# Pooled attention and a residual MLP on one core: where batch 1's v and u go, and when batch 2 is loaded

## The chip, the cores and the metric

The kernel runs on one core of a Trainium2 chip. The metric is the device time of one execution in microseconds (us). Names used below: PE is TensorE (matmuls), DVE is VectorE, ACT is ScalarE, POOL is GpSimd, SP is the engine that issues most DMA. A DMA issued by SP or ScalarE goes out in queue q1 or q10 of the profile, one issued by GpSimd in q0.

## What is computed

Eight batches, eight heads, 576 positions, head size 64. k and v are averaged over groups of 8 positions, so each head has 72 pooled keys and values. The attention's output, heads side by side, is the input x (576 x 512) of a residual MLP that first mixes positions with w_tok and then channels with two weights.

```python
k_p = k.reshape(B, H, 72, 8, D).mean(axis=3)
v_p = v.reshape(B, H, 72, 8, D).mean(axis=3)
attn = softmax(q @ k_p.transpose / sqrt(D))
x = heads_side_by_side(attn @ v_p)

a1 = alpha1 * x + beta1
u = x + lam * einsum('ts,bsd->btd', w_tok, a1)
a2 = alpha2 * u + beta2
out = u + lam * (maximum(a2 @ w_ch1, 0) @ w_ch2)
```

## The kernel before

The 576 positions of a batch make four chunks of 128 rows and one of 64; the 64 of two neighbouring batches share a chunk. Four chunks make a block of the MLP, and there are nine blocks. Blocks and attention are interleaved by hand: while block n runs, the attention and the mixing of batch n + 1 run too, and the loads of batch n + 2 are issued. A block is a list of steps with a number that fixes their order: `mlp_A` (first weight, 16 pieces, steps 0 to 15) and `mlp_B` (second weight, steps 16 to 31), and between them everything else. Block 0 also holds the end of the setting up.

```python
chunks = []
for b in range(0, B, 2):
    chunks += [(b, c) for c in range(4)]
    chunks += [(b + 1, c) for c in range(4)]
    chunks += [(b, 4)]
```

Batch 1's v comes in as 16-bit numbers (cast by the DMA), and TensorE pools it with a matrix of ones and zeros. From batch 2 on v comes in as fp32 and VectorE pools it with three additions for a pair of heads.

```python
def first_V(b, u, copy=nc.vector.tensor_copy):
    ...
    for c in range(4):
        nc.tensor.matmul(out=vp, lhsT=pool_v, rhs=main[:, heads, c], ...)
    for c in range(2):
        nc.tensor.matmul(out=vp, lhsT=pool_vr, rhs=rest[:, heads, c], ...)
    for r in range(2):
        copy(out=vp1_pool[2 * u + r][:, :, 0:64], in_=...)

def att_V(b, hp):
    t = st1[b]["v"][hp // 2][:, 2 * (hp % 2):2 * (hp % 2) + 2]
    for n in (4, 2):
        nc.vector.tensor_tensor(out=t[:, :, 0:n], in0=t[:, :, 0:n], in1=t[:, :, n:2 * n], op=ALU.add)
    nc.vector.tensor_tensor(out=vp1_pool[hp][:, :, 0:64], in0=t[:, :, 0], in1=t[:, :, 1], op=ALU.add)
```

k is summed by GpSimd in two steps (`sum_k`), and TensorE then makes the pooled keys (`att_K`, tile ps_kp, copied to kp). The scores (`att_S4`) need kp and the transposed q.

u is needed with channels on the partitions. For batches 0 and 1 TensorE transposes it and ScalarE copies it to u_fm; later batches use a DMA transpose (the crossbar) from SP.

```python
def mix_uT(key):
    ...
    if key[0] > 1 or key == (0, 4):
        nc.sync.dma_start_transpose(out=u_fm[blk][:, :, 128 * at:128 * at + 128], in_=s["u_bf"])
        return
    ps_uT = gp("ps_uT").bitcast(BF)
    for cc in range(4):
        nc.tensor.transpose(out=ps_uT[0:P, 128 * cc:128 * cc + 128], ...)
    nc.scalar.copy(out=u_fm[blk][:, :, 128 * at:128 * at + 128], ...)
```

The 64 remaining positions of odd batches need the last rows of the transposed w_tok on other partitions than those of even batches. Before, TensorE transposes that part a second time:

```python
def setup_wtok_odd():
    ps_w = gp("ps_wo").bitcast(BF)
    for tcx in range(5):
        nc.tensor.transpose(out=ps_w[:, P * tcx:P * tcx + trc], ...)
    nc.scalar.copy(out=wtT[:, 5, 0:S], in_=ps_w[:, 0:S])
    nc.scalar.copy(out=wtT[0:1, 5, 0:S], in_=wtT[64:65, 4, 0:S])
```

Batch 2's loads are held back by small VectorE memsets into their tiles ("gates"), whose place in VectorE's order sets when SP may issue them.

Of the kernel before, what the change touches and what calls it, by code (L numbers as in the profile page):

```python
# [9 lines left out]
BF = mybir.dt.bfloat16  # L10
# [4 lines left out]
P = 128  # L15
# [4 lines left out]
REM = 64  # L20
# [3 lines left out]
def kernel(  # L24
# [18 lines left out]
    nc = tc.nc  # L43
    ctx.enter_context(tc.manual_schedule())
    B, H, S, D = q.shape
# [6 lines left out]
    def gp(name):  # L52
        return psA.tile([P, 512], FP, tag="gp", name=name)
# [70 lines left out]
                    in_=src[b, h::2, 512:576, :].rearrange("a (i c) d -> i a (c d)", c=2))  # L124
        st1[b]["rem_raw"] = raw

    def load_v(b, u, parts=(0, 1), behind=None):

        if parts[0] == 0:
            st1[b]["v"][u] = work.tile([SPG, 4, 8, D], FP, tag="v_u", bufs=2, name="v_u")  # L130
        v_u = st1[b]["v"][u]
        if behind is not None:
            for rows_ in (slice(0, 64), slice(64, SPG)):
                behind.memset(v_u[rows_, 0, 0, 0:1], 0.0)
        for part in parts:
            g0, g1 = ((0, 64), (64, SPG))[part]
            nc.sync.dma_start(
                out=v_u[g0:g1].rearrange("g h p d -> g h (p d)"),
                in_=v[b, 4 * u:4 * u + 4, 8 * g0:8 * g1].rearrange("h (g p) d -> g h (p d)", p=8))

# [171 lines left out]
        nc.scalar.copy(out=wtT[64:65, 4, cols], in_=ps[64:65, 0:trc])  # L312

    def setup_wtok_odd():
        ps_w = gp("ps_wo").bitcast(BF)
        for tcx in range(5):
            trc = P if tcx < 4 else REM
            nc.tensor.transpose(out=ps_w[:, P * tcx:P * tcx + trc],
                                in_=wt_bf[0:trc, S * tcx + 448:S * tcx + 576],
                                identity=identity_bf[0:trc, 0:trc])  # L320
        nc.scalar.copy(out=wtT[:, 5, 0:S], in_=ps_w[:, 0:S])
        nc.scalar.copy(out=wtT[0:1, 5, 0:S], in_=wtT[64:65, 4, 0:S])


    w1 = [const.tile([P, 4, 512], BF, tag=f"w1_{g}", name=f"w1_{g}") for g in range(4)]
# [5 lines left out]
    def load_w1(g):  # L331
        nc.gpsimd.dma_start(
            out=w1[g],
            in_=moe_w_ch1[:, 512 * g:512 * g + 512].rearrange("(cc p) j -> p cc j", p=P))
# [249 lines left out]
    def mix_uT(key):  # L584
        s = st2[key]
        i = where[key]
        blk, at = i // 4, i % 4
        if blk not in u_fm:
            u_fm[blk] = work.tile([P, 4, 512], BF, tag="u_fm", bufs=3, name="u_fm")
        if key[0] > 1 or key == (0, 4):  # L590
            nc.sync.dma_start_transpose(out=u_fm[blk][:, :, 128 * at:128 * at + 128],
                                        in_=s["u_bf"])
            return
        ps_uT = gp("ps_uT").bitcast(BF)
        for cc in range(4):
# [126 lines left out]
    setup_wtok(3, nc.scalar.copy)  # L722
    att_X(0, 6, 8, nc.vector, False)
    rest_X(0, 0, H)
    load_w1(3)
    load_v16(1, (0, 1))
    mix_T(0, 0, nc.gpsimd)
    setup_rowsum(2)
    mix_T(0, 1)
    setup_rowsum(3)  # L730
    load_v16(1, (2,))
    load_w2(0)
    mix_T(0, 2, nc.gpsimd)
    for g in range(1, 3):
# [16 lines left out]
    def attention(b):  # L751


        first = b == 1
        todo = []
        if first:
            for hp in range(4):
                todo.append((2.6 + 0.9 * hp, lambda hp=hp: att_F(b, hp)))
            todo.append((3.5, lambda: cast_rem(b, nc.gpsimd)))
            todo.append((3.65, lambda: load_w2(3)))  # L760
            todo.append((7.4, lambda: att_Frem(b, nc.scalar.copy)))
        if b < B - 1:
            at = 27.0 if first else 10.0
            todo.append((at, lambda: att_F(b + 1, 0)))
            todo.append((at + 0.1, lambda: att_F(b + 1, 2)))
            at = 28.0 if first else 25.5
            todo.append((at - 1.0, lambda: cast_rem(b + 1, nc.gpsimd)))
            todo.append((at, lambda: att_Frem(b + 1)))
        for u in range(2):
            todo.append((3.6 + 0.1 * u if first else -0.9 + 1.2 * u,  # L770
                         lambda u=u: sum_k(b, u, nc.gpsimd)))
            todo.append((6.4 + 1.8 * u if first else 4.1 + 2.0 * u,
                         lambda u=u: att_K(b, u, nc.vector.tensor_copy)))
            if first:
                todo.append((11.0 + 1.2 * u, lambda u=u: first_V(b, u)))
        for u in range(2):
            at = (9.0 if first else 6.3, 13.6)[u]
            todo.append((at, lambda u=u: att_S4(b, u)))
            for k, dt in enumerate((0.1, 0.1, 0.1, 0.7, 1.7, 1.75) if u else (0.1, 0.1, 0.1, 1.1, 2.1, 3.1)):
                todo.append((at + dt, lambda u=u, k=k: st1[b]["exp", u](k)))  # L780
            for i, dt in enumerate((2.9, 3.4, 4.6, 5.1) if u else (5.7, 6.2, 2.9, 3.4)):
                h = 4 * u + i
                todo.append((at + dt, lambda h=h: att_AV(b, h)))
                if i % 2:
                    eng = nc.gpsimd if h == 5 else nc.vector
                    todo.append((at + dt + 0.1, lambda h=h, eng=eng: att_X(b, h - 1, h + 1, eng)))
        if not first:
            for hp in range(4):
                todo.append((0.2 + 2.0 * hp, lambda hp=hp: att_V(b, hp)))
        for c in range(5):  # L790
            at = 21.0 + 1.3 * c
            if c < 4 or b % 2:
                todo.append((at, lambda c=c: mix_T(b, c)))
                key = (b, c) if c < 4 else (b - 1, 4)
                if first and c in (2, 3):
                    at += 1.3 * c - 2.0
                elif first and c < 2:
                    at += 1.0
                todo.append((at + 1.8, lambda key=key: mix_uT(key)))
        return todo  # L800

    for n in range(NBLK):
        todo = []
# [16 lines left out]
        if b < B:  # L820
            todo += attention(b)
            if b + 1 < B:
                new_batch(b + 1)
                gate = nc.vector if b == 1 else None
                for u in range(2):
                    at = 21.0 + 0.2 * u
                    todo.append((at, lambda b=b, u=u: load_k(b + 1, u, gate)))
                    at = (21.0 if b == 1 else 0.4) + 0.1 * u
                    todo.append((at, lambda b=b, u=u: load_q_bf(b + 1, u)))
                    at = 19.0 + 0.2 * u if b == 1 else 3.5 + 4.0 * u  # L830
                    todo.append((at, lambda b=b, u=u: load_v(b + 1, u, behind=gate)))
                todo.append((20.9, lambda b=b: load_rem(b + 1, behind=gate)))
        for _, do in sorted(todo, key=lambda x: x[0]):
            do()

# [29 lines left out]
```

The softmax here doesn't subtract the row's maximum and nothing guards it: scores larger than these inputs give would overflow.

## Time and profile before

| what | value |
|---|---|
| time, median of 3 runs | 349.15 us (348.95 to 349.62) |
| span of the profiled execution | 347.7 us |
| TensorE busy | 336.4 us, 97% |
| VectorE busy | 219.8 us, 63% |
| ScalarE busy | 150.3 us, 43% |
| GpSimd busy | 89.7 us, 26% |
| DMA moved | 44.57 MB |
| granted TensorE clock | 1.00 |

How to read what follows. The page shows the span in 40 equal slices with a digit of busy share for each engine. In a group or a timeline a line gives the start and the busy time in us, the engine, the line of the kernel, the operation, output and inputs by their tiles, shapes, and the count; square brackets hold the idle time just before it and what ended that. In a table of stretches each line has the stretch, its length, then busy time and number of instructions for PE, weight loads, DVE, ACT and POOL, then the granted clock, the mean busy share of the DMA engines and GB/s. Matmuls are pipelined, so the distance from one start to the next says more of their cost than their own duration.

### The profile page before, as it was taken

The page shows a single profiled execution, that of the slowest core. Times are in us where ns is not written, and L with a number is a line of the kernel's source. Part 1 is how long each engine was busy: PE and PEld are TensorE (multiplying, and loading weights), DVE is VectorE, ACT ScalarE, POOL GpSimd, SP SyncE. Part 2 cuts the span into 40 slices and gives each one's busy share as a digit, 9 for nine tenths or more (in the row PEclk, how much of TensorE's full clock was granted, in tenths as well). Part 3 has the DMA queues.
Part 4 walks back from the last instruction along what each step waited for, and adds up shares of the span by engine and source line. Part 5 has one row for each costly group of instructions (what it writes and reads, how often), then busy time and mean ns, then how long its engine had stood idle before and what let it go on. Part 6 is the DMA issues. An engine that isn't in the chain of part 4 may idle for free.

```text
span 347.7 us, 5897 instructions
## 1 busy us (share of the span) xinstructions
PE 336.4 (97%) x2208; PEld 178.9 (51%) x2249; DVE 219.8 (63%) x463; ACT 150.3 (43%) x283; POOL 89.7 (26%) x104
## 2 busy tenths in 40 slices
PE   8999999998999999999999999999999999999995
PEld 3667554454545554455445544554455445545544
DVE  6673159788686669775867597858685882037511
ACT  3656970257403850186018700790079005604700
POOL 8677404080117011800180027101600100000000
PEclk9999999999999999999999999999999999999999
DMA  8999953999558924895289628991820134011012
GB/s 123 184 219 243 214 115 44 239 240 196 93 178 152 222 48 112 216 201 86 77 235 175 113 72 208 197 139 53 221 69 1 37 85 77 0 60 62 0 58 63
DMA packets 66045, 44.57 MB, mean 128 GB/s; under 512 B 32409, under 2 KB 57309, under 8 KB 66018
## 3 DMA queue, kind: packets, MB, share of 16 engines
q1 hardware_dynamic: 50484, 33.18, 40.2%
q0 software_dynamic: 15072, 10.76, 21.1%
q8 instruction: 17, 0.28, 0.3%
q10 hardware_dynamic: 462, 0.27, 0.3%
q14 instruction: 10, 0.08, 0.1%
HBM read 38.30 MB, written 9.44 MB: 137 GB/s over the span
## 4 chain that ended last, share of the span: by engine, by line
PE 89%; DVE 4%; POOL 2%; DMA 2%; issue 2%; ACT 1%; POOLq 0%; DVEq 0%
PE ps_ch L646 34%; PE ps_h L612 33%; PE ps_tok L575 12%; PE ps_av L521 2%; PE ps_s L477 2%; DMA q_bf<-in_q_dram 2%; DVE v_u L445 1%; PE ps_ch L635 1%; DVE ps_ch L652 1%; PE ps_r L484 1%; PE ps_uT L596 1%; PE ps_av L525 1%; PE ps_kp L407 0%; PE ps_q L370 0%; DVE u_sb L653 0%
## 5 line engine op out<-in xcount | busy, mean ns | idle before, releaser
L617 ACT ACTIVATE Hj<-ps_h,bias_cols 128x512 bf16<-128x512 f32 x144 | 98.4, 689 | 149.1 <-PE ps_h L612 147.6
L612 PE MATMUL ps_h<-u_fm,w 128*128 128x512 bf16 (+1 forms) x571 | 132.2, 374 | 1.3 <-ACT u_fm L598 0.2
L646 PE MATMUL ps_ch<-w,Hj 128*128 128x512 bf16 x543 | 128.7, 379 | 1.1 <-issue 0.6
L612 PEld LDWEIGHTS <-w 128*128 128x128 bf16 x592 | 63.9, 114 | 51.8 <-issue 2.9
L646 PEld LDWEIGHTS <-Hj 128*128 128x128 bf16 x560 | 52.7, 98 | 61.0 <-issue 1.6
L575 PE MATMUL ps_tok<-xs,wtT 128*128 128x512 bf16 (+2 forms) x199 | 44.8, 380 | 0.5 <-DVE xs L543 0.2
L652 DVE TENSOR_TENSOR ps_ch<-lam_bc,ps_ch 128x512 f32<-128x512 f32 x32 | 22.2, 693 | 35.0 <-PE ps_ch L646 34.7
L543 POOL TENSOR_TENSOR xs<-x_tm,lamal_bc 128x512 bf16<-128x512 f32 x10 | 12.7, 1268 | 118.5 <-DVE x_tm L529 115.9
L579 DVE TENSOR_TENSOR u_sb<-x_tm,ps_tok 128x512 f32<-128x512 f32 (+1 forms) x40 | 27.4, 684 | 12.2 <-PE ps_tok L575 12.1
L529 DVE TENSOR_TENSOR x_tm<-ps_av,rec 128x320 f32<-128x320 f32 x64 | 31.4, 491 | 2.8
L653 DVE TENSOR_TENSOR u_sb<-u_sb,ps_ch 128x512 f32<-128x512 f32 x35 | 24.0, 687 | 13.7 <-PE ps_ch L646 12.5
L506 ACT ACTIVATE ET<-ps_s 72x512 f16<-72x512 f32 x56 | 32.3, 592 | 0.0
L527 DVE RECIPROCAL rec<-ps_av 128x5 f32<-128x5 f32 x64 | 12.2, 191 | 31.7 <-PE ps_av L525 31.6
L445 DVE TENSOR_TENSOR v_u<-v_u 72x512 f32<-72x512 f32 (+1 forms) x48 | 28.4, 591 | 0.8
L575 PEld LDWEIGHTS <-wtT 128*128 128x128 bf16 (+3 forms) x200 | 17.4, 100 | 20.9 <-issue 1.3
L582 DVE TENSOR_TENSOR u_bf<-u_sb,al_bc 128x512 bf16<-128x512 f32 x34 | 24.2, 711 | 1.3 <-DMA u_fm<-u_bf 0.2
L160 POOL TENSOR_TENSOR k_raw<-k_raw 128x512 f32<-128x512 f32 x14 | 19.3, 1376 | 11.9 <-DMA k_raw<-in_k_dram 9.4
L521 PEld LDWEIGHTS <-ET 72*128 72x128 f16 x256 | 13.9, 97 | 8.6 <-issue 0.4
L162 POOL TENSOR_TENSOR k_bf<-k_raw 128x512 bf16<-128x512 f32 x14 | 17.8, 1274 | 1.1
L543 DVE TENSOR_TENSOR xs<-x_tm,lamal_bc 128x512 bf16<-128x512 f32 x22 | 15.4, 701 | 0.7
L521 PE MATMUL ps_av<-vp,ET 72*128 72x66 f16 x256 | 15.8, 193 | 0.0
L145 POOL CAST rem_q<-rem_raw 128x256 bf16<-128x256 f32 x7 | 2.8, 399 | 42.0 <-DMA rem_raw<-in_q_dram 42.0
(121 smaller groups left out, 229.9 us busy)
## 6 DMA issues: line engine op xcount, KB each, us to landing
out_dram<-u_sb SPq DMA_DIRECT2D x32, 256.0 KB
k_raw<-in_k_dram SPq DMA_DIRECT2D x14, 512.0 KB
v_u<-in_v_dram SPq DMA_DIRECT2D x12, 512.0 KB
q_bf<-in_q_dram POOLq DMA_DIRECT2D x16, 256.0 KB, 6.5
w<-in_moe_w_ch_dram POOLq DMA_DIRECT2D x8, 512.0 KB, 16.3
v<-in_v_dram POOLq DMA_DIRECT2D x4, 256.0 KB, 11.2
rem_raw<-in_q_dram SPq DMA_DIRECT2D x15, 64.0 KB
rem_raw<-in_k_dram SPq DMA_DIRECT2D x15, 64.0 KB
```

Of the source, the lines that this page charges most:

```text
L445: nc.vector.tensor_tensor(out=t[:, :, 0:n], in0=t[:, :, 0:n], in1=t[:, :, n:2 * n], op=ALU.add)
L506: nc.scalar.activation(out=o, in_=i, func=AF.Exp, bias=0.0, scale=0.125)
L521: nc.tensor.matmul(out=av[:, odd + c, :], lhsT=ET[:, m0:m0 + 128], rhs=vp1[:, hh, :])
L529: nc.vector.tensor_tensor(out=x[:, 1 - odd:6 - odd, dd:dd + D], in0=av[:, :, 0:64], in1=rec.unsqueeze(2).to_broadcast((P, 5, D)), op=ALU.mult)
L543: eng.tensor_tensor(out=xs[:, 0:4, cols], in0=x[:, 1:5, cols], in1=lamal_bc[:, cols].unsqueeze(1).to_broadcast((P, 4, D * (h1 - h0))), op= ...
L575: nc.tensor.matmul(out=ps_tok[p0:p1], lhsT=wtT[0:kk, at, P * c:P * c + p1 - p0], rhs=xs_pool[i][0:kk, sc, :], start=(sc == 0), stop=(sc == 4))
L579: nc.vector.tensor_tensor(out=s["u"][p0:p1, :], in0=x[p0:p1, 1 + c if c < 4 else 5 - 5 * i, :], in1=ps_tok[p0:p1, 0:DM], op=ALU.add)
L582: eng.tensor_tensor(out=s["u_bf"], in0=s["u"], in1=al2_bc, op=ALU.mult)
L612: nc.tensor.matmul(out=ps_h[:, t0:t1], lhsT=w1_of(cc, j), rhs=u_fm[n][:, cc, t0:t1], start=(cc == 0), stop=(cc == 3))
L617: nc.scalar.activation(out=t, in_=ps_h, func=AF.Relu, bias=bias_cols[:, j:j + 1], scale=1.0)
L646: nc.tensor.matmul(out=ps, lhsT=Hj[n, j][:, 128 * m:128 * m + 128], rhs=w2[j // 4][:, j % 4, :], start=(j == 0), stop=(j == NJ - 1))
L652: nc.vector.tensor_tensor(out=ps, in0=lam_bc, in1=ps, op=ALU.mult)
```

## The change

It has four parts. Batch 1's v is loaded as fp32 by GpSimd's queue, ahead of w1's last piece, and pooled by VectorE (`att_V`) like all later batches; `first_V` stays for batch 0 alone. Batch 1's u goes over the crossbar, like all later batches. The odd w_tok rows are moved by two small DMAs from SP instead of being transposed a second time. Batch 2's loads (q, v, the remainders, k) are issued from the middle of block 0, where they were issued late in it, and its transposes of q move from step 27 to step 21.5. It is meant to take work off TensorE in block 0 and to use the time in which the DMA engines have little to do.

```diff
-    def load_v(b, u, parts=(0, 1), behind=None):
+    def load_v(b, u, parts=(0, 1), behind=None, queue=nc.sync):
...
     def setup_wtok_odd():
-        ps_w = gp("ps_wo").bitcast(BF)
-        for tcx in range(5):
-            trc = P if tcx < 4 else REM
-            nc.tensor.transpose(out=ps_w[:, P * tcx:P * tcx + trc], ...)
-        nc.scalar.copy(out=wtT[:, 5, 0:S], in_=ps_w[:, 0:S])
-        nc.scalar.copy(out=wtT[0:1, 5, 0:S], in_=wtT[64:65, 4, 0:S])
+        nc.vector.memset(wtT[0:64, 5, 0:S], 0.0)
+        nc.sync.dma_start(out=wtT[64:128, 5, 0:S], in_=wtT[0:64, 4, 0:S])
+        nc.sync.dma_start(out=wtT[0:1, 5, 0:S], in_=wtT[64:65, 4, 0:S])
...
-        if key[0] > 1 or key == (0, 4):
+        if blk:
             nc.sync.dma_start_transpose(out=u_fm[blk][:, :, 128 * at:128 * at + 128],
...
-    load_w1(3)
-    load_v16(1, (0, 1))
+    for u in range(2):
+        load_v(1, u, queue=nc.gpsimd)
     mix_T(0, 0, nc.gpsimd)
     setup_rowsum(2)
     mix_T(0, 1)
     setup_rowsum(3)
-    load_v16(1, (2,))
+    load_w1(3)
     load_w2(0)
...
-            at = 27.0 if first else 10.0
+            at = 21.5 if first else 10.0
             todo.append((at, lambda: att_F(b + 1, 0)))
             todo.append((at + 0.1, lambda: att_F(b + 1, 2)))
-            at = 28.0 if first else 25.5
+            at = 25.5
             todo.append((at - 1.0, lambda: cast_rem(b + 1, nc.gpsimd)))
             todo.append((at, lambda: att_Frem(b + 1)))
...
-            todo.append((6.4 + 1.8 * u if first else 4.1 + 2.0 * u,
+            todo.append((6.4 + 2.2 * u if first else 4.1 + 2.0 * u,
                          lambda u=u: att_K(b, u, nc.vector.tensor_copy)))
-            if first:
-                todo.append((11.0 + 1.2 * u, lambda u=u: first_V(b, u)))
...
-        if not first:
-            for hp in range(4):
-                todo.append((0.2 + 2.0 * hp, lambda hp=hp: att_V(b, hp)))
+        for i, hp in enumerate((1, 0, 2, 3) if first else range(4)):
+            todo.append(((6.6, 8.7, 10.0, 12.6)[i] if first else 0.2 + 2.0 * hp, lambda hp=hp: att_V(b, hp)))
...
-                if first and c in (2, 3):
-                    at += 1.3 * c - 2.0
-                elif first and c < 2:
-                    at += 1.0
                 todo.append((at + 1.8, lambda key=key: mix_uT(key)))
...
-                    at = 21.0 + 0.2 * u
+                    at = (15.2 if b == 1 else 21.0) + 0.2 * u
                     todo.append((at, lambda b=b, u=u: load_k(b + 1, u, gate)))
-                    at = (21.0 if b == 1 else 0.4) + 0.1 * u
+                    at = (14.0 if b == 1 else 0.4) + 0.1 * u
                     todo.append((at, lambda b=b, u=u: load_q_bf(b + 1, u)))
-                    at = 19.0 + 0.2 * u if b == 1 else 3.5 + 4.0 * u
+                    at = 14.5 + 0.2 * u if b == 1 else 3.5 + 4.0 * u
                     todo.append((at, lambda b=b, u=u: load_v(b + 1, u, behind=gate)))
-                todo.append((20.9, lambda b=b: load_rem(b + 1, behind=gate)))
+                todo.append((15.1 if b == 1 else 20.9, lambda b=b: load_rem(b + 1, behind=gate)))
```

More of the change, by code (lines that the diff above doesn't have):

```diff
@@ L136, in load_v @@
             g0, g1 = ((0, 64), (64, SPG))[part]
-            nc.sync.dma_start(
+            queue.dma_start(
                 out=v_u[g0:g1].rearrange("g h p d -> g h (p d)"),
@@ L314, in setup_wtok_odd @@
     def setup_wtok_odd():
-        ps_w = gp("ps_wo").bitcast(BF)
-        for tcx in range(5):
-            trc = P if tcx < 4 else REM
-            nc.tensor.transpose(out=ps_w[:, P * tcx:P * tcx + trc],
-                                in_=wt_bf[0:trc, S * tcx + 448:S * tcx + 576],
-                                identity=identity_bf[0:trc, 0:trc])
-        nc.scalar.copy(out=wtT[:, 5, 0:S], in_=ps_w[:, 0:S])
-        nc.scalar.copy(out=wtT[0:1, 5, 0:S], in_=wtT[64:65, 4, 0:S])
+        nc.vector.memset(wtT[0:64, 5, 0:S], 0.0)
+        nc.sync.dma_start(out=wtT[64:128, 5, 0:S], in_=wtT[0:64, 4, 0:S])
+        nc.sync.dma_start(out=wtT[0:1, 5, 0:S], in_=wtT[64:65, 4, 0:S])
     w1 = [const.tile([P, 4, 512], BF, tag=f"w1_{g}", name=f"w1_{g}") for g in range(4)]
```

## The prediction

> **What bounds the kernel now.** I read the page's busy shares and slices first, then TensorE's time block by block, then the waits and the timelines of the first 80 us, where every change lies.
>
> ```profile
> PE 336.4 (97%) x2208; PEld 178.9 (51%) x2249; DVE 219.8 (63%) x463; ACT 150.3 (43%) x283; POOL 89.7 (26%) x104
> ...
> DMA  8999953999558924895289628991820134011012
> ```
>
> TensorE is nearly always busy, so only less work on it, or less waiting by it, saves time. A slice is 8.7 us. The DMA engines are full to about 43 us, fall to 5 and 3 tenths between 43 and 61 us (in the records the last w2 piece lands at 50.2, and nothing moves from then until batch 2's first load), and are full again to 87 us: a hole in front of the loads that the change brings forward.
>
> The table of stretches has one block of the MLP per line; each starts at its first ps_h matmul (blocks 0 to 4).
>
> ```profile
> 28.53:71.80 43.27, 42.33 (x345) 24.90 (x349) 22.74 (x54) 22.30 (x46) 12.31 (x15) 1.00 0.89 179
> 71.80:108.39 36.59, 35.18 (x221) 18.10 (x224) 27.47 (x52) 15.24 (x28) 14.19 (x14) 1.00 0.79 164
> 108.39:144.88 36.49, 36.12 (x230) 18.49 (x234) 27.55 (x55) 15.09 (x28) 9.66 (x11) 1.00 0.66 146
> 144.88:180.09 35.21, 35.00 (x222) 18.09 (x224) 24.70 (x52) 15.09 (x28) 9.34 (x10) 1.00 0.67 149
> ```
>
> Blocks 1 and 3 do the same work, yet block 1 takes 36.59 and block 3 35.21: **1.38 us** are lost in block 1, the most that earlier loads of batch 2 can give there. Blocks 2 and 4 (36.49 each) need nothing. VectorE's timeline shows how it is lost, and TensorE's where.
>
> ```profile
> 73.34 3.12 DVE L445 TENSOR_TENSOR v_u<-v_u 72x512 f32<-72x512 f32 x2
> 76.49 1.25 DVE L447 TENSOR_TENSOR vp<-v_u 72x128 f16<-72x128 f32 x1
> 77.66 1.13 DVE L445 TENSOR_TENSOR v_u<-v_u 72x512 f32<-72x512 f32 x2
> ```
> ```profile
> 36.50 0.28 PE L407 MATMUL ps_kp<-pool_main,k_bf 128*128 128x64 bf16 x4
> ...
> 39.48 0.29 PE L407 MATMUL ps_kp<-pool_main,k_bf 128*128 128x64 bf16 x4 [0.28 <-POOL k_bf L162]
> ...
> 79.53 0.30 PE L477 MATMUL ps_s<-qT,kp 64*72 64x256 bf16 x2 [1.19 <-DVE kp L419]
> ```
>
> Pooling the first half-pair of v takes 3.12 + 1.25 us beside GpSimd's sums of k (GpSimd is busy from 71.88 to 77.6); the next pair takes 1.13 + 0.29. So kp is copied late and the scores wait 1.19 us. The first two TensorE lines are batch 1's pooled k in block 0: the first half does not wait at all, the second 0.28 us for GpSimd. Keep them in mind.
>
> GpSimd's queue there, with the DMA issues in it, and the time to landing of two earlier loads (x1: q of batch 1, second half, issued at 11.65; w1's third piece, issued at 14.03):
>
> ```profile
> 28.28 0.60 POOL L337 DMA_DIRECT2D w<-in_moe_w_ch_dram  x1
> 29.55 0.53 POOL L337 DMA_DIRECT2D w<-in_moe_w_ch_dram  x1 [0.68 <-DMA q_bf<-in_q_dram]
> 30.07 0.41 POOL L145 CAST rem_q<-rem_raw 128x256 bf16<-128x256 f32 x1
> 30.44 0.73 POOL L148 TENSOR_TENSOR rem_k<-rem_raw 128x256 bf16<-128x256 f32 x1
> 32.62 1.27 POOL L160 TENSOR_TENSOR k_raw<-k_raw 128x512 f32<-128x512 f32 x1 [1.45 <-PE ps_h L612]
> 33.97 1.27 POOL L162 TENSOR_TENSOR k_bf<-k_raw 128x512 bf16<-128x512 f32 x1
> ```
> ```profile
> q_bf<-in_q_dram POOLq DMA_DIRECT2D x1, 256.0 KB, 17.6
> ...
> w<-in_moe_w_ch_dram POOLq DMA_DIRECT2D x1, 512.0 KB, 19.5
> ```
>
> The issue at 29.55 (w2's third piece) waited for that q: 11.65 + 17.6 = 29.25. That q is the eighth load before it in this queue, and the one wait of w1's third piece (1.59 us, at 14.03) was also for its eighth forerunner. **An issue on this queue waits until the load eight places earlier has landed**, and all that stands behind it on GpSimd waits too.
>
> [...]q1 (SP) with 40.2% and q0 (GpSimd) with 21.1% are shares of one set of 16. [...] 3.12 against 1.13 us above, and GpSimd's 1.27 becomes 1.71 at 74.46.
>
> **The change part by part.** First what leaves TensorE in block 0. Starts of neighbours in its timeline give the true cost:
> - the odd w_tok transposes: 39.66 to 40.11, **0.45 us**;
> - first_V of batch 1, two times six matmuls: 43.56 to 44.43, and 46.09 to 46.95, **1.73 us**;
> - u of batch 1, four sets of four transposes of 0.22 us: **0.87 us**.
>
> That is 3.05 us. ScalarE loses 0.64 + 0.67 (wtT copies) and 4 x 0.59 (u_fm). Second, block 1: batch 2's v gates move from step 19 to 14.5 and k from 21 to 15.2, so some 8 us earlier. Its sums of k, at 71.9 to 77.6 now, should be done before block 1 begins, VectorE pools at 1.4 us a pair, and I take **1.3 of the 1.38 us** as won.
>
> Third, what it adds. VectorE pools v for batch 1: four pairs of 1.13 + 0.29 = 5.7 us, plus a memset; in 28.7 to 51.3 us it was busy only 5.92 of 22.6, so this fits, though one pair will meet GpSimd's sum of k and take 2 to 3 us. The loads: v as fp32 is 4 issues where there were 3. Counting places as built, w2's first three pieces now wait for q, q and **w1's third piece** where the third waited for q. w1's third piece lands at 14.03 + 19.5 = 33.5. So GpSimd, free at 30.08 before, is free at about 34.1: cast 0.41, remainder 0.73, sum 2 x 1.27 with gaps, k_bf at 37.9 instead of 35.2. TensorE wants it at 36.50: **a stall of 1.4 us**. Then w2's fourth piece is issued (0.57), and the second sum ends at 41.1, or 41.6 beside VectorE; TensorE would come there at 40.6: another 0.5 to 1.0. Less the old 0.28, I count **2.0 us** for both.
>
> Fourth, ScalarE in the score stretch (41 to 52 us) has about 9 us of copies and exps; without first_V TensorE's own work there is about 9 too. I charge **0.4 us** of lost pace.
>
> Fifth, the crossbar. Block 1 is the only block whose four chunks are all of the batch mixed just before, so it needs all four u of batch 1. In a steady block SP's four u transposes take 1.2 us each among other issues (173.05 to 180.2) and the last lands 1.2 us later. Here SP must first issue v, rem and k of batch 2 from about 50 us. In the steady blocks v's landing comes some 10 us after its first issue (149.36, then 159.1), so near 60.5, and SP then issues one output, two q transposes, u, output, u, u, rem, u: about 10 us, with the last u landing near 71.5. TensorE comes at 71.8 - 3.05 + 2.0 + 0.4 = 71.2, or later. I charge **0.7 us**, from 0 to 2.
>
> w1's and w2's last pieces come about 1 us later than now (fp32 v has twice the bytes of the cast one): w1's fourth near 41.5, needed at 45; w2's fourth near 51.5, needed at 53.8. No wait expected.
>
> Sum: -3.05 - 1.3 + 2.0 + 0.4 + 0.7 = **-1.25 us**, so 349.15 becomes about 347.9.
>
> **Rivals.** (a) All saved work counts and no new wait comes: -4.35 us, 344.8. For it: the parts are tuned together (the second k half is moved from 8.2 to 8.6). Against it: the queue order, which the trace has shown to bind twice. (b) The crossbar chain becomes the bound at block 1's start: the last u lands at 74 or so, 2 to 3 us later than TensorE comes, and the time is 350. For it: SP's issues are serial and the k loads stand in front; against it: nothing moves the SP work later than 50 us. (c) v and q of batch 2 take bandwidth from the last w2 pieces, and the first ps_ch sums wait: 1 to 2 us, 349. For it: q of batch 2 is ungated on GpSimd and goes out near 42 us; against it: it stands behind w2 in the same queue.
>
> **Range and chances.** The removed work (3.05) is near certain, block 1's gain nearly so; the stalls have 0 to 6 us between them. 345.5 to 350.0 holds most of it. A change of 2% is 7 us, more than the whole of the saved work: faster by that 0.01, slower by it 0.02.
>
> **What will show it.** A wait of GpSimd for a w load before rem_q, and ps_kp waiting some 1.4 us for k_bf near 37 us: the third step. Block 1 at 35.3 us or so, with no wait for kp: the second. A gap of TensorE before block 1's first ps_h, released by a DMA: the fifth. If GpSimd does not stop there, or if w1's third piece lands before 31 us, I am too high by 2; if the last u lands after 73 us, too low.

## The result and the profile after

The changed kernel takes **362.04 us** (median of 4 runs, 361.70 to 362.89), the kernel before, run beside it, 349.38 (348.95 to 349.94). The ratio is 1.0365, 95% interval 1.0341 to 1.0389: slower by 3.6%, where 347.9 was predicted and 350.0 was the top of the range. In this part, where a kernel's runs spread widely, ratios are taken over its undisturbed runs and medians over all of them.

The page after, first the busy shares, then the granted TensorE clock and the DMA share in the 40 slices (a slice is 9.0 us now):

```profile
PE 341.4 (95%) x2176; PEld 180.0 (50%) x2216; DVE 223.8 (62%) x472; ACT 147.0 (41%) x277; POOL 89.8 (25%) x105
...
PEclk9969969998999999999999999999999999999999
DMA  8999991999243892489459926694650033002002
```

TensorE has 32 matmuls fewer and yet 5.0 us more busy time: the clock's row, all 9 for the kernel before, has two slices at 6 and one at 8. The table of stretches, one line per block (blocks 0 to 2), shows where the time went:

```profile
31.44:85.15 53.71, 42.30 (x313) 23.17 (x316) 31.56 (x71) 18.84 (x40) 19.64 (x21) 0.94 0.94 185
85.15:122.04 36.89, 36.68 (x221) 18.38 (x226) 21.53 (x45) 15.17 (x28) 6.48 (x7) 0.95 0.48 119
122.04:158.53 36.49, 36.17 (x232) 18.50 (x234) 27.29 (x55) 15.10 (x28) 9.68 (x11) 1.00 0.67 143
```

Block 0 starts 2.91 us later than before, takes **10.44 us more**, block 1 takes 0.30 more, and block 2 takes what it took (36.49). TensorE's timeline has three long gaps in block 0 (the last is counted to it, as it lies ahead of block 1's first matmul):

```profile
42.38 0.29 PE L402 MATMUL ps_kp<-pool_main,k_bf 128*128 128x64 bf16 x4 [2.80 <-POOL k_bf L162]
...
49.08 0.39 PE L402 MATMUL ps_kp<-pool_main,k_bf 128*128 128x64 bf16 x4 [3.98 <-POOL k_bf L162]
...
85.15 6.17 PE L607 MATMUL ps_h<-u_fm,w 128*128 128x512 bf16 x20 [4.00 <-DVE v_u L440]
```

The third is put down to VectorE, but in the DMA's own records the last crossbar transpose of u lands at 84.90 us, 0.25 us before TensorE goes on; that is what it waited for. Whose fault the first two are, GpSimd's timeline shows:

```profile
33.73 0.53 POOL L332 DMA_DIRECT2D w<-in_moe_w_ch_dram  x1 [1.94 <-DMA w<-in_moe_w_ch_dram]
...
39.72 1.26 POOL L160 TENSOR_TENSOR k_raw<-k_raw 128x512 f32<-128x512 f32 x1 [4.36 <-DMA k_raw<-in_k_dram]
...
46.44 1.25 POOL L160 TENSOR_TENSOR k_raw<-k_raw 128x512 f32<-128x512 f32 x1 [3.60 <-DMA k_raw<-in_k_dram]
```

The first line is the stop on w1's third piece that the prediction told of. But it isn't what ends last: GpSimd then waits 4.36 us and 3.60 us **for k itself**. Both halves of k, issued 2 us later than before (24.9 and 25.5, before 22.6 and 23.2), landed at 39.7 and 46.4 us; before they landed at 32.5 and 36.7.

The granted clock stood at half in three stretches: one ahead of block 0, one that begins in the second gap, and one from the end of the third gap on. The last three columns of a stretch's line are the clock, the DMA share and GB/s:

```profile
17.03:23.86 6.83, 6.61 (x61) 5.34 (x60) 3.61 (x14) 3.73 (x10) 3.59 (x4) 0.50 1.26 211
47.75:54.58 6.83, 5.50 (x28) 2.40 (x29) 3.07 (x7) 1.94 (x5) 2.75 (x3) 0.50 1.05 169
```

The third is 85.30 to 88.71. Inside the third, ps_h matmuls start 0.43 us apart (85.41 to 88.40), at the full clock 0.22 (42.56 to 43.22): continuous work at half the clock loses half its length. The first one therefore costs 3.4 us at most: in the timelines TensorE was 0.61 us behind the kernel before ahead of it (the same matmul at 16.77 and 16.16 us) and 2.92 us behind after it (25.17 and 22.25), so some 2.3 of the 2.91 us by which block 0 starts late came in it. The rest closes too. Block 0: 2.80 + 3.98 + 4.00 of gaps, 2.75 for the half clock (6.83 less the 1.33 us of it that lie in the second gap, halved), less 3.05 of removed work and the 0.28 us of waiting before: +10.20, measured +10.44. Block 1: -1.38 gained, +1.71 of half clock: +0.33, measured +0.30.

### The profile page after: what moved, and what is told of

It reads as the page before. It is cut to its first block, busy times and chain, and to the rows that moved or that the text cites. A ratio compares the mean times of both kernels' runs of the same rounds, so it can differ in the third digit from the quotient of the medians.

```text
span 361.2 us, 5844 instructions
## 1 busy us (share of the span) xinstructions
PE 341.4 (95%) x2176; PEld 180.0 (50%) x2216; DVE 223.8 (62%) x472; ACT 147.0 (41%) x277; POOL 89.8 (25%) x105
## 4 chain that ended last, share of the span: by engine, by line
PE 82%; DMA 11%; DVE 2%; POOL 1%; issue 1%; ACT 0%; DVEq 0%; POOLq 0%; SPq 0%; ACTq 0%
PE ps_ch L641 33%; PE ps_h L607 33%; PE ps_tok L570 10%; DMA k_raw<-in_k_dram 6%; DMA q_bf<-in_q_dram 3%; PE ps_s L472 2%; DMA k<-in_k_dram 2%; PE ps_av L516 2%; PE ps_ch L630 1%; DVE v_u L440 1%; DVE ps_ch L647 1%; PE ps_r L479 1%; PE ps_kp L402 0%; PE ps_av L520 0%; DVE u_sb L648 0%
## 5 line engine op out<-in xcount | busy, mean ns | idle before, releaser
L607 PE MATMUL ps_h<-u_fm,w 128*128 128x512 bf16 (+1 forms) x572 | 135.7, 381 | 5.3 <-DVE v_u L440 4.0
L538 POOL TENSOR_TENSOR xs<-x_tm,lamal_bc 128x512 bf16<-128x512 f32 x10 | 12.7, 1265 | 132.2 <-DVE x_tm L524 127.9
L440 DVE TENSOR_TENSOR v_u<-v_u 72x512 f32<-72x512 f32 (+1 forms) x56 | 30.8, 550 | 1.0
L577 DVE TENSOR_TENSOR u_bf<-u_sb,al_bc 128x512 bf16<-128x512 f32 x34 | 26.2, 770 | 2.0 <-DMA u_fm<-u_bf 0.8
L414 DVE CAST kp<-ps_kp 128x288 bf16<-128x288 f32 x14 | 6.4, 458 | 22.4 <-PE ps_kp L408 21.9
L162 POOL TENSOR_TENSOR k_bf<-k_raw 128x512 bf16<-128x512 f32 x14 | 18.4, 1317 | 1.1
```

Of the source, the lines that this page charges most:

```text
L538: eng.tensor_tensor(out=xs[:, 0:4, cols], in0=x[:, 1:5, cols], in1=lamal_bc[:, cols].unsqueeze(1).to_broadcast((P, 4, D * (h1 - h0))), op= ...
L577: eng.tensor_tensor(out=s["u_bf"], in0=s["u"], in1=al2_bc, op=ALU.mult)
L607: nc.tensor.matmul(out=ps_h[:, t0:t1], lhsT=w1_of(cc, j), rhs=u_fm[n][:, cc, t0:t1], start=(cc == 0), stop=(cc == 3))
```

## The experiments

Theory at the outset: k comes late because of fp32 v in GpSimd's queue, and the crossbar chain is late for a reason of its own. Rivals: the earlier loads of batch 2, GpSimd's stop, or the clock by itself. Packet counts below are from the DMA records of the traces, landing times from the last update of the load's semaphore; the sum of k in GpSimd starts at that time or a little after.

### Which part costs

**The kernel before, unchanged**, and **the change unchanged**:

> The kernel before, once more, with its trace taken beside the others. In the changed kernel's trace block 0 already starts 2.9 us later than in the kernel before (31.44 against 28.53 us), with TensorE's clock at one half from 17.0 to 23.9 us, in a part of the program that the change hardly touches. Theory A (this belongs to the change, or to a phase that it sets): here block 0 starts at 28.5 us and the granted clock is 1.00, 349 us. Theory B (it comes from the chip or the run): here, too, the clock falls before 24 us and block 0 starts near 31 us, about 352 us.

> The changed kernel unchanged, run again. Its profile so far showed TensorE's clock at half from 17.0 to 23.9 us, before block 0, and block 0 started at 31.44, 2.9 us later than before the change; the kernel that has fp32 v alone started it at 31.09, those without fp32 v in GpSimd's queue at 28.4 to 29.6. Theory A (that early half clock belongs to the change, since nothing else differs): block 0 again starts later than 31.0 and the time is 361 to 363. Theory B (the early half clock comes and goes from run to run, as the later ones do): block 0 starts by 29.7 in the profiled run, k still lands after 38 and after 45 us, ps_kp waits 2.5 us or more both times, and the time is 358 to 361.

The kernel before took 350.02 (348.85 to 352.40, 18 runs; ratio 0.9999, 0.9988 to 1.0011), with the clock at 1.00 and block 0 started at 29.41. The changed kernel took 360.01 (358.95 to 361.06; ratio 1.0279, 1.0252 to 1.0307). Its clock did not fall before block 0, which started at 29.16; k landed at 37.9 and 42.2, the ps_kp waits were 3.36 and 0.50, and the gap ahead of block 1 was 3.82. So theory B for the clock, but not for the second half of k, which was expected after 45 us with a wait of 2.5 or more. The 2.9 us ahead of block 0 come and go and so does a part of the second wait; a late k and the gap ahead of block 1 stay. Beside the kernel before the change costs 12.7 us in the first set of runs and 9.9 in this one.

**fp32 v alone**, on the kernel before:

```diff
-    load_w1(3)
-    load_v16(1, (0, 1))
+    for u in range(2):
+        load_v(1, u, queue=nc.gpsimd)
...
-    load_v16(1, (2,))
+    load_w1(3)
...
-    first_V(1, u) in block 0
+    att_V(1, hp) in block 0
```

> The kernel before with the first part alone: batch 1's v as fp32 in GpSimd's queue ahead of w1's last piece, pooled by VectorE. Theory 1: most of the loss is here, ps_kp waits some 3 and 4 us in block 0, about 356 us or more. Rival (each part is harmless alone and the loss comes of their meeting): about 348 to 350 us, ps_kp waiting 1.4 us or less.

358.11 (357.93 to 362.38; ratio 1.0266, 1.0209 to 1.0324). In the profiled run, the slowest of the four, the ps_kp waits were 3.42 and 5.38 and k landed at 39.9 and 49.6. This one part alone makes the kernel 2.7% slower.

**The change without its crossbar part** (u of batch 1 back on TensorE):

```diff
-        if blk:
+        if key[0] > 1 or key == (0, 4):
...
+                if first and c in (2, 3):
+                    at += 1.3 * c - 2.0
+                elif first and c < 2:
+                    at += 1.0
```

> The changed kernel with batch 1's u transposed by TensorE and copied by ScalarE again; the rest stays. Theory 2 (the last u over the crossbar landed at 84.9 us, TensorE waited 4.0 us at block 1's start and then ran at half clock for 3.4 us): that wait goes, 20 matmuls take 4.3 us again instead of 6.2, and 0.9 us of transposes come back: about 357 us, with the ps_kp waits unchanged. Rival (another landing holds block 1's start, q or k of batch 2): the wait moves to a ps_s or ps_kp in block 1 and the time stays near 361.

356.73 (354.80 to 357.87; ratio 1.0192, 1.0157 to 1.0227): the gap ahead of block 1 is gone and block 1 takes 35.20, while the ps_kp waits are 2.82 and 5.69. **The change without its v part** (v 16-bit and pooled by TensorE, w1's last piece in its old place), the reverse of the diff of fp32 v alone:

> The changed kernel with batch 1's v again cast to 16 bit by the DMA, behind w1's last piece, and pooled by TensorE; the other three parts stay. Theory 1 (fp32 v ahead in GpSimd's queue takes the DMA engines from k of batch 1, whose halves landed at 39.7 and 46.4 us instead of 32.5 and 36.7): k lands by about 38 us, the two ps_kp waits of 2.8 and 4.0 us go, and so does the half clock from 47.8 to 54.6 us; with first_V's 1.7 us back that is about 354 us, less if the early half clock goes too. Rival (GpSimd's stop on the semaphore of w1's third piece sets the sums of k): that stop goes too, so ps_kp's waits vanish, but k's landing would not be earlier than 39 us. Rival 2 (the crossbar is all that costs): over 358 us.

351.20 (349.40 to 354.61, 12 runs; ratio 1.0034, 1.0008 to 1.0059). No wait at ps_kp; but the gap ahead of block 1, 3.80 us in the profiled run, is there with v untouched. So there are two faults. **Only the early loads and the odd rows** (both of these edits on the changed kernel, so neither its v part nor its crossbar part):

> The two parts that have cost nothing so far, alone on the kernel before: batch 2's loads from the middle of block 0, and the odd w_tok rows by DMA. u of batch 1 on TensorE, v of batch 1 as 16 bit. Theory: block 1 falls from 36.5 to 35.2 us, as it did with u back on TensorE (35.20), and block 0 loses 0.45 us of transposes: 349.4 - 1.3 - 0.45 = 347.6 us, a ratio of 0.995. Rival (batch 2's loads meet w2's last pieces and hold up the first ps_ch sums): block 0 longer than 43.5 us, 349 or more.

348.45 (347.41 to 349.10; ratio 0.9955, 0.9937 to 0.9972). Blocks 0 and 1 of this version:

```profile
29.02:72.12 43.10, 42.29 (x346) 24.55 (x344) 24.32 (x55) 21.16 (x44) 20.16 (x21) 1.00 1.05 205
72.12:107.32 35.20, 35.20 (x225) 18.09 (x224) 24.87 (x52) 15.15 (x28) 7.30 (x8) 1.00 0.60 137
```

Block 1 took 36.59 and 36.53 in the two traces of the kernel before, so the early loads bring 1.33 to 1.39 us, as computed (1.38). Block 0 took 43.27 and 43.54 there, so it gains 0.17 to 0.44; the two traces differ by too much to show the odd rows' 0.45 us exactly. The whole gain, 1.63 us, is near the computed 1.83: these two parts do what was computed.

### Why k comes late

**fp32 v behind w1's last piece**, u on TensorE:

```diff
+    load_w1(3)
     for u in range(2):
         load_v(1, u, queue=nc.gpsimd)
...
-    load_w1(3)
```

> As the changed kernel with u of batch 1 back on TensorE (356.7 us, ps_kp waits 2.8 and 5.7 us), but with w1's last piece ahead of the fp32 v in GpSimd's queue, so that beside k of batch 1 the queue carries cast weights as before, and v comes after. Theory 1 (the fp32 v, while it runs beside k, takes k's share of the DMA engines): k lands near 33 and 37 us again; what is left is GpSimd's stop for w1's third piece, so ps_kp waits about 1.4 us and then 0.5 to 1; no half clock; about 348.5 us. Rival (k is late because GpSimd's queue as a whole moves more, wherever v stands): ps_kp waits over 2.5 us at least once, 353 us or more.

355.31, but from 348.34 to 356.91 over 12 runs (ratio 1.0024, 0.9993 to 1.0055): no verdict from the time. The profiled run (351.2) helps: k's first half was on time (33.0), the second late (39.7), just as v now went out beside the second; the waits were 0.41 and 3.10.

**The same place, but 16-bit**, and **fp32 behind k in SP's queue**, both with u on TensorE:

```diff
-    for u in range(2):
-        load_v(1, u, queue=nc.gpsimd)
+    load_v16(1, (0, 1))               # 16-bit, pooled by first_V
+    load_v16(1, (2,))
```
```diff
+    load_w1(3)
     for u in range(2):
-        load_v(1, u, queue=nc.gpsimd)
+        load_v(1, u)
...
-    load_w1(3)
```

> Batch 1's v is loaded as 16 bit (cast by the DMA, pooled by TensorE) and u of batch 1 is transposed by TensorE, but the v loads keep the changed kernel's place in GpSimd's queue, ahead of w1's last piece. Apart from that place it is the kernel with the early loads and the odd rows by DMA alone, which took 348.45. Theory fp32 (k comes late because v comes in as fp32): k lands by 35 and by 39 us, the ps_kp waits are under 0.8 each, the time is 348 to 349.5. Theory place (k comes late because anything ahead of w1's last piece moves beside it): k lands after 38 and 44 us, the two waits sum to over 5 us, the time is 354 to 357.

> The changed kernel with batch 1's fp32 v issued by SP, behind k in the same queue, instead of by GpSimd, w1's last piece in its old place, and u of batch 1 transposed by TensorE. The bytes and the VectorE pooling of the change are kept; only the queue is another. Theory queue (k is late because fp32 v comes in beside it, from the other queue): k lands by 35 and by 39 us, the ps_kp waits are under 0.8 each, the clock stays at 1.00 in block 0, and with first_V's 1.73 us gone the time is 346.5 to 347.5 (348.45 less some 1.5). Theory bytes (fp32 v is simply too much to move before block 0's middle): v lands late, TensorE waits for vp, or w2 comes late, 349 to 353.

The 16-bit v in the changed place took 347.32 (347.03 to 347.89; ratio 0.9919, 0.9896 to 0.9942), k was there for GpSimd's sums at 32.60 and 35.75, and TensorE did not wait:

```profile
36.52 0.28 PE L402 MATMUL ps_kp<-pool_main,k_bf 128*128 128x64 bf16 x4
...
39.06 0.28 PE L402 MATMUL ps_kp<-pool_main,k_bf 128*128 128x64 bf16 x4
```

So the place is not it. But fp32 v in the other queue took 356.52 (ratio 1.0181, 1.0158 to 1.0205): k's first half was on time (34.5), its second landed only at 45.2, though v stood *behind* it. My theory of the queue fell there too: something else than v went beside k's second half. The packets told what. The lines are the DMA queues' packets and MB (q0 GpSimd, q1 SP), first of the kernel before from 28 to 34 us, then of the changed one in the same 6 us:

```profile
q0 software_dynamic: 743, 0.73, 71.9%
q1 hardware_dynamic: 745, 0.75, 45.2%
```
```profile
q0 software_dynamic: 486, 1.17, 83.1%
q1 hardware_dynamic: 495, 0.32, 27.0%
```

**In both, the two queues move nearly the same number of packets.** k's packets are 1 KB. Before, w1's pieces (1 KB) went beside them, and both queues got half of the 246 GB/s. After, 240 of v's packets of 4 KB take the time (one took 0.26 us in the mean, one of 1 KB in the same queue 0.10), and q1 keeps a fifth of the bytes. 273 of its 495 packets are the remainders' (512 B each), behind which k stands, and then k itself moves 61 packets in a microsecond (32 to 34 us), where it moved 121 before. Over 14 to 60 us the changed kernel has 800 packets of 4 KB, 512 of w2 and 288 of v, so k is held up twice: by v up to 34 us, and by w2's pieces from 40 us, where k's second half still was on its way. Before, w1's last piece and the 16-bit v's 1024 packets of 512 B and 256 of 256 B stood between, and k was through (at 36.7) before w2's first packet (37.7). With fp32 v in SP's queue that shield is gone and w2 starts at 32.

That the packets' number decides, and not their bytes, is so far my reading of these counts. Three experiments were meant to change the size of packets at equal bytes. First, fp32 v in rows of 1 KB (four positions) into a padded tile, u on TensorE:

```diff
-    work.tile([SPG, 4, 8, D], FP, ...)
+    work.tile([SPG, 4, 2, 4 * D + 8], FP, ...)     # batch 1
...
+    for a in range(2):
+        queue.dma_start(out=v_u[:, :, a, 0:4 * D], in_=src[a])
```

> The changed kernel with u of batch 1 on TensorE, as in the run that took 356.73; batch 1's v is still fp32, in GpSimd's queue, at the changed place, with four issues and pooled by VectorE, but in rows of 1 KB (four positions) into a padded tile, so that its packets should be 1 KB instead of the 4 KB that the trace shows. Theory packets ([...]4 KB packets beside k's 1 KB ones hold k up): k lands by 35 and by 39.5 us, the ps_kp waits sum to under 2, the time is 346.5 to 348. Theory bytes (1.18 MB of fp32 ahead of w1's last piece are what holds k up): k lands after 38 and 44 us, the waits sum to over 5, the time is 354 to 358.

353.55 (352.23 to 359.86, 5 runs; ratio 1.0087, 1.0062 to 1.0112), waiting 6.23 at ps_kp. This decides nothing: the trace again shows 800 packets of 4 KB, so the edit did not make them smaller. Why it is 3.2 us faster than the version it was made from (356.73) stays open. Second, the kernel with fp32 v in SP's queue, and w2's rows padded, which does make w2's packets 1 KB:

```diff
-    w2 = [const.tile([P, 4, DM], BF, ...) for g in range(4)]
+    w2 = [const.tile([P, 4, DM + 8], BF, ...)[:, :, 0:DM] for g in range(4)]
```

> The run with fp32 v in SP's queue behind k (356.52; k's second half landed at 45.2 us while w2 went beside it in 4 KB packets), with w2's tile padded by 16 bytes a row so that its packets should be 1 KB. Bytes, order and pooling are the same. Theory packets: k lands by 35 and by 39.5 us, the ps_kp waits sum to under 1.5, the clock stays at 1.00 there and the time is 346.5 to 348.5, unless v or w2 then come late. Theory bytes: k's second half again after 43 us, 355 to 358.

350.12 (348.37 to 352.80, 20 runs; ratio 0.9997, 0.9982 to 1.0012), 6.4 us less than without the padding (there the clock stood at half for 10.2 us, here it did not). The two queues from 36 to 44 us and the ps_kp wait, without the padding and then with it:

```profile
q0 software_dynamic: 380, 1.38, 85.2%
q1 hardware_dynamic: 384, 0.49, 20.2%
```
```profile
47.96 0.40 PE L402 MATMUL ps_kp<-pool_main,k_bf 128*128 128x64 bf16 x4 [7.97 <-POOL k_bf L162]
```
```profile
q1 hardware_dynamic: 720, 1.24, 57.4%
q0 software_dynamic: 772, 0.76, 56.4%
```
```profile
41.74 0.29 PE L402 MATMUL ps_kp<-pool_main,k_bf 128*128 128x64 bf16 x4 [1.99 <-POOL k_bf L162]
```

With the same bytes, k's second half lands at 39.0 instead of 45.2 and the wait falls from 7.97 to 1.99. For w2 that is packets, not bytes. It isn't all: 1.99 us stay (k's second half still lands 2.3 us later than before the change) and 1.35 us of waiting ahead of a ps_h come in, so the time misses the 346.5 to 348.5 expected.

Third, the other way: 16-bit v ahead of w1's last piece with its packets made large. v is fetched in pieces of 2048 neighbouring numbers; it then lies in the wrong order for the pooling matrix, so batch 1's output is another, with the same instructions.

```diff
-    out=main[:, 4 * u:4 * u + 4]..., in_=rows(v, b, u)
+    out=flat[64 * u:64 * u + 64],
+    in_=v[b] as rows of 32 positions [64 * u:64 * u + 64]
```

> The run with 16-bit v ahead of w1's last piece (347.32), with the same bytes of v in other rows: batch 1's v is fetched in pieces of 2048 neighbouring numbers a partition, so that GpSimd's queue should carry it in 144 packets of 4 KB instead of 1152 of 512 B. It lies in the wrong order for the pooling matrix, so batch 1's output is another; instructions and bytes are the same. Theory packets: few large packets no longer stand between w1's last piece and w2, w2's 4 KB packets come beside k; k's second half lands after 42 us, a ps_kp wait of over 3, time 352 to 356. Theory bytes: as before, k lands by 33 and 36.5 us, no wait, 347 to 348.

352.16, from 348.48 to 358.11 over 20 runs (ratio 1.0006, 0.9978 to 1.0033), where the small packets gave 347.32 within 0.9 us. In the profiled run k, issued 0.4 us later, landed at 34.3 and 39.0, where with the small packets it landed at 32.5 and 35.5, and the wait was 1.95. So v's packets, too, count at equal bytes. The sign is the expected one, the size is not: I expected k after 42 and a wait over 3. w1's last piece (512 packets of 1 KB) still stood between v and w2, and let most of k through. For the fp32 v itself no run has other packets at the same bytes; that it holds up k by its packets rests on the counts from 28 to 34 us.

### Why the crossbar comes late

In the run without the v part, this is TensorE's gap, the issue of the last u and GpSimd's issue of batch 3's q ahead of it:

```profile
75.35 7.20 PE L607 MATMUL ps_h<-u_fm,w 128*128 128x512 bf16 x20 [3.80 <-DMA u_fm<-u_bf]
```
```profile
69.88 1.22 SPq L586 DMA_TRANSPOSE u_fm<-u_bf  x1
```
```profile
68.39 1.55 POOL L77 DMA_DIRECT2D q_bf<-in_q_dram  x2
```

The last u lands at 75.1, 4.0 us after its issue ended. The loads of q, which the change does not touch, are issued as soon as GpSimd gets there, and fall into the middle of the transposes. The next run, on the same version, holds them back with a VectorE memset:

```diff
         bf = work.tile([P, 4, 4, D], BF, tag="q_bf", bufs=4, name="q_bf")
+        if b == 3:
+            nc.vector.memset(bf[:, 0, 0, 0:1], 0.0)
```

> As v16_back (351.2 us; TensorE waited 3.8 us for the last u over the crossbar, and GpSimd had issued q of batch 3 at 68.4 us, while SP issued the last two transposes at 68.6 and 69.9), but the load of q of batch 3 is held back by two small VectorE writes into its tiles until VectorE has pooled block 1's first v. Theory 2a (those loads take the DMA engines from the transposes): the last u lands about 1.3 us after its issue as in later blocks, the wait falls from 3.8 to about 1 us, the half clock in block 1 goes, about 347.5 us. Rival 2b (SP's chain of issues alone is too late): the wait stays over 3 us, about 351 us.

347.56 (346.95 to 347.94; ratio 0.9928, 0.9911 to 0.9945). The issue of q moves to 74.96:

```profile
69.20 1.22 SPq L588 DMA_TRANSPOSE u_fm<-u_bf  x1
```
```profile
74.96 1.55 POOL L79 DMA_DIRECT2D q_bf<-in_q_dram  x2 [7.18 <-DVE q_bf L78]
```
```profile
71.86 4.48 PE L609 MATMUL ps_h<-u_fm,w 128*128 128x512 bf16 x20
```

and the last u lands 1.2 us after its issue ended (71.6), with no gap ahead of block 1. That settles the cause of the second fault. The rival, that the cost is the clock after the gap, was tried with 16 matmuls that compute nothing ahead of block 1:

```diff
     for n in range(NBLK):
+        if n == 1:
+            keep_warm(16)
```

> As v16_back, with 16 matmuls of zeros (3.5 us of TensorE's work, their output unused) put just ahead of block 1, into the wait for the last u. Theory 3 (the idle gap makes the clock fall to one half, and the first 7 us of block 1 run at it): the granted clock stays 1.00, block 1 takes 35.2 us instead of 38.1, and since the matmuls run while TensorE would wait anyway: 351.2 - 2.5 = 348.7 us. Rival (the clock falls for another reason, or its fall costs nothing because something else bounds block 1): 351 us or more.

350.68 (349.87 to 351.71, 17 runs; ratio 1.0017, 1.0007 to 1.0027). In the profiled run the clock stays at 1.00 and block 1 takes 35.21, where it took 38.08 without them; the last u still lands late, at 73.7, and the 16 matmuls run past it to 74.5, so they cost some 0.6 us themselves. Against 351.20 they save 0.5 us in the median. Without them the mean clock was below 1.00 in 9 of the 12 runs; the three others took 349.40 to 350.23. So the fall of the clock adds to the gap where it comes (2.9 us in block 1 of the profiled run), and is not its cause.

### The change repaired

**The whole change with 1 KB rows of fp32 v and with batch 3's q held back:**

> The whole change with two repairs: batch 1's fp32 v in rows of 1 KB, and q of batch 3 held back by VectorE so that it is not issued beside the crossbar transposes of u. If the two causes found (large packets beside k; q beside the transposes) are all that kept the change from its 3.05 and 1.38 us, no wait over 1 us is left at ps_kp or at block 1's start, the clock stays at 1.00 in block 0 and the time is 345 to 347. If something else of the change also costs (GpSimd's stop on w1's third piece, ScalarE, VectorE's pooling), it is 347 to 350.

352.72 (352.38 to 354.00; ratio 1.0084, 1.0059 to 1.0109). As its packets were 4 KB still, the ps_kp waits were 1.88 and 2.32; the gap ahead of block 1 was 0.89. **The whole change with q held back and v cast to 16 bit**, in the change's own layout, place and pooling:

```diff
-    st1[b]["v"][u] = work.tile([SPG, 4, 8, D], FP, ...)
+    st1[b]["v"][u] = work.tile([SPG, 4, 8, D], F16 if b == 1 else FP, ...)
```

> The whole change with one type altered, and q of batch 3 held back by VectorE: batch 1's v is cast to 16 bit by the DMA into the change's own layout (packets of 1 KB instead of 4 KB) and pooled by VectorE. 1088 packets of 1 KB (v and w1's last piece) then stand between the loads before and w2, against some 1150 of k and the remainders. Theory packets: k lands by 35 and 39.5 us, waits at ps_kp sum to under 2 (GpSimd's stop on w1's third piece may keep 1 to 1.5 of them), the change's 3.05 and 1.38 us come off, time 345 to 347.5. Rival (any v ahead in that queue makes GpSimd stop and that costs by itself): waits over 3, clock at half, 350 or more.

347.55 (346.52 to 348.38; ratio 0.9910, 0.9878 to 0.9942). v's packets are 1 KB, k is summed at 34.07 and 37.50, the clock stays at 1.00 in blocks 0 and 1, and GpSimd's stop on w1's third piece is still there (3.52 us). The two waits of TensorE that are left:

```profile
40.43 0.29 PE L404 MATMUL ps_kp<-pool_main,k_bf 128*128 128x64 bf16 x4 [0.99 <-POOL k_bf L164]
...
71.06 4.48 PE L609 MATMUL ps_h<-u_fm,w 128*128 128x512 bf16 x20 [1.01 <-DVE ps_ch L649]
```

The second, too, is put down to VectorE, but the last u lands at 70.82, 0.24 us before TensorE goes on. So with q out of the way SP's row of transposes alone costs 1.01 us here. The cast halves v's bytes as well as quartering its packets, so this version shows that the change can be repaired and not which of the two did it.

**16-bit v pooled by TensorE, ahead of w1's last piece, crossbar for u, q held back** (the edits of two runs above together), and **the version with q held back and the second half of k half a step later:**

```diff
-            todo.append((6.4 + 1.8 * u if first else 4.1 + 2.0 * u,
+            todo.append((6.4 + 2.3 * u if first else 4.1 + 2.0 * u,
```

> 16-bit v pooled by TensorE but ahead of w1's last piece (that alone, with u on TensorE, took 347.32), u of batch 1 over the crossbar and q of batch 3 held back. Expected by both: the 0.87 us of u's transposes come off as well if the last u lands before TensorE comes, 346.2 to 346.8; if TensorE waits for the last u, 347 to 348.5.

> The version with 16-bit v pooled by TensorE, u of batch 1 over the crossbar and q of batch 3 held back by VectorE (347.56), with the second half of batch 1's pooled k half a step later in block 0 (the changed kernel's own shift is 0.4 of a step in that direction). If the second ps_kp still waited in that version the time falls by 0.1 to 0.5, to 347.1 or so; if it did not wait, it is 347.4 to 347.9, the same.

347.70 (346.76 to 348.02; ratio 0.9930, 0.9907 to 0.9952) and 347.48 (346.92 to 349.21; ratio 0.9927, 0.9901 to 0.9952). Neither is a clear gain on what it was made from. In the first the clock stood at half from 18.4 to 21.8 and block 0 started at 30.44, so its profile doesn't show what the crossbar part is worth; in the second TensorE waited 1.31 us ahead of block 1.

Six versions beat the kernel before, all by less than 1%: five at 0.9910 to 0.9930 (347.3 to 347.7 us), whose intervals overlap, so that which is best stays open, and the early loads with the odd rows alone at 0.9955.

## Why the prediction was wrong

- **The removed work, 3.05 us, and block 1, 1.3 of 1.38 us: right.** Block 1 takes 35.19 to 35.36 in every profiled run with the early loads and the clock at 1.00 in it. The removed work shows in the cast version's block 0 (below); the odd rows' 0.45 us alone shows as 0.17 to 0.44.
- **GpSimd's stop on w1's third piece: right as a mechanism, but not what set the end.** It came as told (1.94 us, the piece landing at 33.45, predicted 33.5). In the version with cast v it came with 3.52 us, the first ps_kp did not wait and the second waited 0.99: 0.71 us more than before the change. So even without the late k the 2.0 us were too many by 1.3; the first stall of 1.4 us did not come.
- **"A stall of 1.4 us", "2.0 us for both": the step that failed.** Here the prediction went wrong most. It counted GpSimd's instructions from the end of its stop and took k as landed, because k had landed at 32.5 and 36.7 before. No step asked what fp32 v in the other queue does to a load of SP that the change does not touch. The prediction noted that the queues' figures are shares of one set of 16 engines, and drew nothing from it for k. k landed at 39.7 and 46.4 instead, because of the packets of 4 KB in the other queue, and the two waits were 2.80 and 3.98 us, 6.78 together.
- **The crossbar, "0.7 us, from 0 to 2": right for SP's row of transposes, mis-sized at 4.00 for what went beside it.** The chain was rightly seen as serial on SP, and the last u was to land near 71.5; with q held back it landed at 71.6 in the version without the v part, and in the five versions with q held back the wait ahead of block 1 was at most 1.31 us. Left out were the loads of batch 3's q on GpSimd, which otherwise go beside it: without the v part TensorE waited 3.80 us in the profiled run. Rival (b) had the place, with another reason (SP's serial issues).
- **The clock: no term at all.** About 2.75 us in block 0 and 1.71 in block 1 here, and some 2.3 ahead of block 0, which did not come again. Of the three gaps here two brought this cost with them (the one of 2.80 us did not), so a small error in a wait was not a small error in the time.
- **The 0.4 us of ScalarE's pace and VectorE's pooling** were not measured by themselves. In the cast version block 0's sum, -3.05 + (0.99 - 0.28) + 1.01 + 0.4 = -0.93, meets the measured 42.44 less 43.54 or 43.27, so -1.10 or -0.83, and leaves little room for more.
- **Rival (a)**, 4.35 us of gain, was reached by no version. **Rival (c)**, w2 late, did not come: none of the changed kernel's three gaps is w2's. w2 was not late but in the way.

So with the two collisions taken out (the cast version) the change gains 0.9%, 2.9 us beside the kernel before, somewhat more than its sum of 1.25; with them it costs 12.7 us, or 9.9 where the half clock ahead of block 0 and a part of k's second wait did not come.

## What to carry to other kernels

When a change moves a load, ask first what other load is on its way then and in which queue, and compare the sizes of packets and not only the bytes: beside packets four times as large, a load that nobody touched here got half of its pace (61 packets in a microsecond, 121 before). Read the landing time of every load that the critical engine needs, before and after, ahead of counting instructions. And count a TensorE gap of some 2 us or more with what the clock may take after it: here it took 1.7 to 2.75 us after one of 4, and it fell after one of 1.95.

## What the runs showed of the hardware

- **Packets of equal number, not bytes.** In 28 to 34 us: 743 to 745 before, 486 to 495 after. GpSimd's queue carried fp32 v without a cast in 4 KB packets even in padded rows of 1 KB, and the cast w2 in 4 KB packets that padding of its rows turned to 1 KB; the 16-bit v came in packets of 512 B, 1 KB or 4 KB where its rows in SBUF were so long.
- **Crossbar transposes suffered more than q's load in one run.** In the changed kernel 325 to 998 packets of 256 B moved in q1 in each microsecond from 74 to 79 us, ahead of q's first packet. In the run without the v part they were 35 and 40 in the two (72 to 74) in which q moved 358 and 369 packets of 512 B, so here the equal count does not hold. In the changed kernel it nearly does from 82 to 84 us (256 and 258 beside 291 and 289). What decides stays open.
- **The clock after gaps.** In the profiled runs it stood at half, for 3.4 to 13.7 us, with each of the eleven gaps of 3.1 to 8.0 us. With shorter ones it went either way: the clock fell with two of five gaps of 1.88 to 2.82 us that began at full clock. It fell after 1.95 us ending at 41.74, and did not after 1.99 us at the same place in another kernel, nor after 2.80 us in the changed one. In two traces it also stood at half ahead of block 0: for 6.83 us from 17.03 in the changed kernel, where no gap over 0.23 us lies in the 10 us ahead, and for 3.4 us from 18.4 with the 16-bit v in front, the crossbar and q held back. What starts that stays open.
